# Rows for columns, an own-step product moved by one slot, and two units of batch two loaded ahead of the last weights, in a fused recurrence and MLP-mixer kernel

## The chip, the cores and the metric

The kernel runs on one core of a Trainium2 chip. The metric is device microseconds of one execution. Executions of one kernel spread: those of the kernel before by 0.6%. Runs are marked slow because they lie over 1.5% above the fastest run of their kernel; the medians below are over all runs of a kernel. Engines: PE multiplies matrices (PEld is its weight load), DVE, ACT and POOL work elementwise, SP issues most transfers. In the profile nearly every line is L68, a helper that issues all operations, so groups are told apart by their tiles.

## The reference, cut to what matters

Four batches, eight heads, 768 steps, head size 48. First a linear recurrence with a decay `w` and a bonus `u` for the own step, then a token mix and a channel mix.

```python
for t in range(S):
    cur = einsum('bhd,bhe->bhde', u * k_t, v_t)
    y[:, :, t] = einsum('bhd,bhde->bhe', r_t, state + cur)
    state = w * state + einsum('bhd,bhe->bhde', k_t, v_t)
x = y.transpose(0, 2, 1, 3).reshape(B, S, H * D)
h = relu(x.transpose(0, 2, 1) @ w_tok1) @ w_tok2
u = x + h.transpose(0, 2, 1)
out = u + relu(u @ w_ch1) @ w_ch2          # w_ch2: 1536 x 384
```

## The kernel before

The recurrence is cut into chunks of 128 steps. A *unit* is one chunk of one batch: units 0 to 5 are batch one, 6 to 11 batch two, and so on. A unit passes four stages, one per *slot*: `p` (elementwise products, on POOL for batch two and later), `a` (transposes), `b` (scores), `c` (output and state). Slot *s* runs `c` of unit *s*-3, `b` of *s*-2, `a` of *s*-1 and `p` of *s*, and each engine works through its instructions in program order. From batch two on, the slots are woven between the channel mix of the batch before: *ups* (u @ w_ch1, 0.5 us each) and *downs* (@ w_ch2, 2 us each).

```python
def load_unit(b, c):                     # k, r, v of one unit, 192 KB each, on SP
    ...
    if (b, c) in after and nm == "kt":   # hold the load back behind this instruction
        tc.add_manual_dep(ins.ins, after[b, c].ins.name, ...)

for q in range(2):                       # decay columns, element by element
    act.dma_start(wd[q * P:q * P + D, :], w.rearrange("(a q) d -> q d a", q=2)[q])
WARM = (10, 2, 1)                        # dummy products that keep PE's clock up
BY_POOL = (3, 5)                         # units of batch one whose kp POOL makes
WEIGHTS_AT = {4: (0,), 5: (1,), 6: (2,), 7: (3, 4)}   # 4 = all of w_ch2
...
def stage_p(b, c):                       # for b > 0: kp, rp, ku, all on POOL
    pool.tensor_mul(kp[:, :, 0:D], h3(kt), h3(wn[:, g, :]))   # kp: one of three buffers
    pool.tensor_mul(L["rp"][:, :, 0:D], h3(rt), h3(wp[:, g, :]))
    pool.tensor_mul(L["ku"], kt, u_bc)
def own_step(L):                         # yd, on POOL; in slot b for b > 0, in slot c for b == 0
    pool.tensor_mul(h3(L["yd"]), h3(L["vb"]), L["adg"]...)
...
after[1, 0] = done[0, C - 1]             # batch two's loads wait for batch one's last output
u1 = ups(0, 1)
items = ups(0, 0, 6) + u1[:6] + downs(0, 0, 0, 1) + u1[6:] + downs(0, 0, 1) + downs(0, 1)
events = [att(0.5, 6), att(4.0, 7)]      # slots 6, 7 at these places among the items
events += [att(8.0 + 3.2 * j, 8 + j) for j in range(7)]
events += mixing(1, 28.5, 31.5, 34.0)
merge(items, fetch([0.0] * 6 + ...) + events)
```

## Time and profile before

| | before |
|---|---|
| time | 185.99 us, median of 3 (185.12 to 186.02) |
| span of the profiled run | 184.1 us |
| batch one's attention ends (last `x_b`) | 31.75 us |
| products of unit 6 can start on POOL in full (`rp`) | 46.48 us |
| POOL's `kp` of unit 9 | 56.33 us |
| POOL's `rp` of unit 13 ends | 74.5 us |
| first up of batch two | 84.43 us |

The chain of waits of the kernel before follows. It is traced back from the last instruction; its columns are start, length, and what ran or was waited for.

```profile
1.74 5.33 DMA wd<-in_w_dram
7.16 0.21 ACT lnwd L68
...
10.07 0.16 PE at_ps_268 L68
...
31.19 0.56 DVE x_b L68
...
32.19 14.15 DMA rt<-in_r_dram
46.48 1.00 POOL rp_661 L68
...
56.37 0.96 POOL kp_139 L68
57.33 0.96 POOL rp_661 L68
58.28 1.12 POOL ku L68
59.52 0.83 POOL yd L68
...
73.23 1.28 POOL rp_663 L68
...
81.94 2.35 DMA uT<-u_sb
...
84.43 1.14 PE z_ps L68 x6
```

The chain has four parts: a start that waits for the decay columns, batch one's attention, 14 us of waiting for r of unit 6, then POOL at four operations per unit (about 4.0 us) until unit 13. After 84 us it is PE nearly without a break.

The list of waits of the kernel before (engine and tile that waited, releaser: total us, times, longest us):

```profile
POOL kp_139 L68 <- DMA kt<-in_k_dram: 11.5, 1, 11.5
...
DVE x_b L68 <- POOL yd L68: 5.6, 5, 1.8
...
POOL rp_661 L68 <- DMA rt<-in_r_dram: 3.1, 1, 3.1
```

Windows of five microseconds of the kernel before (window, its length, busy time and instruction count of PE, PEld, DVE, ACT and POOL, granted PE clock, DMA share, GB/s):

```profile
40.00:45.00 5.00, 3.00 (x21) 1.59 (x18) 0.00 (x0) 3.13 (x8) 0.99 (x1) 1.00 1.27 193
45.00:50.00 5.00, 2.48 (x11) 1.46 (x12) 1.44 (x2) 1.82 (x3) 3.52 (x4) 0.70 0.92 184
```

PE is busy 5.5 of these 10 us, the DMA engines are full, and the clock falls. This gap is what the change aims at: unit 6 lands behind the second channel weights (`w_ch2`), which landed at 46.1 us.

### The profile page before, as it was taken

To read this page: it belongs to the slowest core of one execution; us is meant where nothing else is said; L and a number is where in the kernel's file an instruction comes from. 1 tells how busy PE (TensorE), PEld (TensorE's weight loads), DVE (VectorE), ACT (ScalarE), POOL (GpSimd) and SP (SyncE) were. 2 spreads that over 40 slices of the span, in tenths; PEclk is the share of its full clock that TensorE was granted. 3 is DMA by queue.
4 is the path that set the end of the run, shared out by engine and by line. 5 is a ranking of instruction groups with operands and counts; after the bars stand their busy time and mean duration, and the time that the engine had idled before them with its cause. 6 is when DMAs were issued, how large, how long until landed. Compare 5 with 4: busy or idle time off the path is not lost.

```text
span 184.1 us, 3991 instructions
## 1 busy us (share of the span) xinstructions
PE 165.5 (90%) x1504; PEld 106.8 (58%) x1504; DVE 106.0 (58%) x193; ACT 100.0 (54%) x217; POOL 93.8 (51%) x113
## 2 busy tenths in 40 slices
PE   7788888893699899798999999899999999999992
PEld 2376776461367566465667666666665665656651
DVE  6465877700469999974669977996541071121121
ACT  2695565493578744404959748654645444445500
POOL 5459795002999999943597999991100000000000
PEclk9999999999699999999999999999999999999999
DMA  4999998999999998124699999233011134211212
GB/s 92 185 203 163 191 141 143 196 184 196 187 219 215 234 225 195 45 45 107 136 235 232 189 243 196 44 67 108 0 46 43 43 86 89 85 43 43 85 47 85
DMA packets 90354, 24.44 MB, mean 133 GB/s; under 512 B 83680, under 2 KB 90336, under 8 KB 90336
## 3 DMA queue, kind: packets, MB, share of 16 engines
q1 hardware_dynamic: 86368, 20.85, 54.0%
q0 software_dynamic: 3408, 3.15, 11.0%
q10 hardware_dynamic: 560, 0.20, 0.7%
q8 instruction: 12, 0.20, 0.4%
q14 instruction: 6, 0.05, 0.1%
HBM read 20.84 MB, written 4.72 MB: 139 GB/s over the span
## 4 chain that ended last, share of the span: by engine, by line
PE 58%; POOL 14%; DMA 13%; DVE 6%; ACT 5%; issue 3%; ACTq 0%; SPq 0%; DVEq 0%; POOLq 0%
PE h_ps L68 23%; PE z_ps L68 20%; DMA rt<-in_r_dram 8%; POOL ku L68 3%; POOL yd L68 3%; DMA wd<-in_w_dram 3%; PE tr_ps L68 3%; DMA uT<-u_sb 3%; PE y_ps L68 2%; PE ad_ps L68 2%; POOL rp_661 L68 2%; POOL rp_663 L68 1%; PE hT_ps L68 1%; POOL rp_665 L68 1%; DVE u_sb L68 1%
## 5 line engine op out<-in xcount | busy, mean ns | idle before, releaser
L68 ACT ACTIVATE zr<-z_ps 128x384 bf16<-128x384 f32 x96 | 44.3, 495 | 31.7 <-PE z_ps L68 31.6
L68 PE MATMUL h_ps<-wch_198,zr 128*128 128x384 bf16 x288 | 50.4, 326 | 0.2
L68 PEld LDWEIGHTS <-zr 128*128 128x128 bf16 x288 | 28.0, 98 | 18.9 <-issue 1.0
L68 DVE TENSOR_TENSOR osb<-u_sb,h_ps 128x384 f32<-128x384 bf16 x24 | 13.3, 552 | 44.5 <-PE h_ps L68 44.5
L68 ACT COPY rk<-tr_ps 128x1024 bf16<-128x1024 bf16 x18 | 18.2, 1012 | 19.2 <-PE tr_ps L68 18.7
L68 PE MATMUL z_ps<-uT,wch_0_196 128*128 128x384 bf16 x144 | 27.6, 337 | 1.1 <-DMA uT<-u_sb 1.1
L68 PE MATMUL z_ps<-uT,wch_1_197 128*128 128x384 bf16 x144 | 26.5, 326 | 0.8 <-ACT zr L68 0.6
L68 DVE TENSOR_TENSOR rku<-ku,rt 128x384 f32<-128x384 f32 x18 | 18.6, 1033 | 11.3 <-POOL ku L68 11.3
L68 POOL TENSOR_TENSOR yd<-vb,adg 128x384 f32<-128x384 bf16 x24 | 20.0, 834 | 7.3 <-DVE adg L68 6.7
L68 PEld LDWEIGHTS <-wch_0_196 128*128 128x128 bf16 x144 | 14.0, 101 | 10.4 <-issue 3.2
L68 POOL TENSOR_TENSOR ku<-kt,u_bc 128x384 f32<-128x384 f32 x18 | 20.0, 1110 | 0.0
L68 PEld LDWEIGHTS <-wch_1_197 128*128 128x128 bf16 x144 | 13.8, 98 | 10.1 <-issue 1.7
L68 DVE TENSOR_TENSOR x_b<-y_ps,yd 128x384 bf16<-128x384 f32 x24 | 13.3, 553 | 10.6 <-POOL yd L68 5.6
L68 POOL TENSOR_TENSOR kp_139<-kt,wn 128x384 bf16<-128x384 f32 x7 | 7.0, 999 | 17.2 <-DMA kt<-in_k_dram 11.5
L68 PEld LDWEIGHTS <-rk 48*128 48x128 bf16 (+1 forms) x272 | 11.4, 95 | 6.3 <-issue 3.0
L68 DVE TENSOR_TENSOR u_sb<-x_b,hT_ps 128x384 bf16<-128x384 bf16 x24 | 11.8, 547 | 1.5 <-PE hT_ps L68 1.5
L68 ACT CAST vb<-vt 128x384 bf16<-128x384 f32 x24 | 12.3, 514 | 0.0
L68 DVE TENSOR_REDUCE adg<-rku 128x8 f32<-128x384 f32 x18 | 9.9, 553 | 0.8
L68 PE MATMUL hT_ps<-h1r,wtok_195 128*128 128x384 bf16 x48 | 9.4, 326 | 0.9 <-ACT h1r L68 0.8
L68 PE MATMUL idle_ps<-warm 128*128 128x512 bf16 x20 | 7.8, 520 | 2.2 <-DVE warm L68 1.3
L68 PE MATMUL h_ps<-x_b,wtok_194 128*128 128x384 bf16 x48 | 8.9, 325 | 0.1
L68 POOL TENSOR_TENSOR rp_661<-rt,wp 128x384 bf16<-128x384 f32 x6 | 6.6, 1101 | 3.1 <-DMA rt<-in_r_dram 3.1
(318 smaller groups left out, 253.6 us busy)
## 6 DMA issues: line engine op xcount, KB each, us to landing
kt<-in_k_dram SPq DMA_DIRECT2D x24, 192.0 KB, 3.7
vt<-in_v_dram SPq DMA_DIRECT2D x24, 192.0 KB, 3.9
out_dram<-osb SPq DMA_DIRECT2D x24, 192.0 KB, 1.9
rt<-in_r_dram SPq DMA_DIRECT2D x18, 192.0 KB, 3.9
wch_198<-in_moe_w_ch_dram POOLq DMA_DIRECT2D x1, 1152.0 KB, 17.6
wch_0_196<-in_moe_w_ch_dram POOLq DMA_DIRECT2D x1, 576.0 KB, 8.9
wch_1_197<-in_moe_w_ch_dram POOLq DMA_DIRECT2D x1, 576.0 KB, 10.5
wtok_194<-in_moe_w_tok_dram POOLq DMA_DIRECT2D x1, 384.0 KB, 7.5
```

The lines of the kernel that those rows point to most:

```text
L68: return lambda *args, **kw: tc.keep_in_program_order(f(*args, **kw))
```

## The change

Its intent has three parts. The decay columns come as contiguous rows and one small transpose on PE, and in batch one `kp` goes to DVE and the own-step product `yd` moves into slot `b`, where its sums are made (the *front*). Units 6 and 7 are loaded ahead of the second channel weights, which are cut in two and issued after unit 7's products on POOL; slot times are shifted to suit (the *load order*). Batch two's token mix turns half its chunks by PE instead of by DMA and puts one of two rectified halves on DVE (the *turns*).

```diff
-    for q in range(2):
-        act.dma_start(wd[q * P:q * P + D, :], w.rearrange("(a q) d -> q d a", q=2)[q])
+    act.dma_start(rows_wu[0:HP]..., w.rearrange("(a q) d -> a q d", q=2))
+    act.dma_start(rows_wu[HP:HP + 3], u...)
...
-    WARM = (10, 2, 1)
+    WARM = (4, 4, 2, 1)
...
     keep_warm(WARM[0])
+    pe.transpose(wu_ps, rows_wu, ident_f[0:HP + 3, 0:HP + 3])
+    keep_warm(WARM[1])
...
-    WEIGHTS_AT = {4: (0,), 5: (1,), 6: (2,), 7: (3, 4)}
+    WEIGHTS_AT = {4: (0,), 5: (1,), 6: (2,), 7: (3,)}     # 4, 5: halves of w_ch2
...
-    BY_POOL = (3, 5)
+    BY_POOL = ()
...
             act.copy(L["adg"], ad_ps)
+            own_step(L)                                    # stage b; gone from stage c
...
+        if s == 7:
+            after[1, 0] = done[0, C - 2]
...
-    after[1, 0] = done[0, C - 1]
...
-        hid, bk, _ = token_mix(b)
+        hid, bk, tn = token_mix(b, by_pe=range(3) if b == 1 else ())
...
-    events = [att(0.5, 6), att(4.0, 7)]
-    events += [att(8.0 + 3.2 * j, 8 + j) for j in range(7)]
-    events += mixing(1, 28.5, 31.5, 34.0)
+    events = [att(0.0, 6), att(3.0, 7), (3.1, 0.0, lambda: load_weights((4, 5))), att(6.5, 8)]
+    events += [att(t, 9 + j) for j, t in enumerate((15.5, 19.0, 22.0, 25.0, 27.5, 30.0))]
+    events += mixing(1, 30.5, 32.5, 35.0)
```

## The prediction

> **What bounds the kernel now** (185.99 us, span 184.1)
>
> 1. Prologue: in the chain of waits the decay-column load (4-byte elements) takes 5.3 us; its logarithm starts at 7.16 us, the first score matmul at 10.0.
> 2. Batch one's attention, to 31.75 us: slots of about 3.7 us. The waits list puts DVE 5.6 us behind the own-step product `yd` on POOL, which stands behind the next unit's `m` and so behind the loads of r (landing near 6.9, 9.9, 12.9, 15.9, 19.5, 22.8 us). Windows show the DMA engines full.
> 3. 42.6 to 47.5 us: PE nearly idle (waits: POOL 11.5 us on k of unit 6, 3.1 on r). Unit 6 lands at 46.3 us, behind the second channel weights (46.1); the granted clock then falls to 0.5 for 3.4 us.
> 4. 46.5 to 74.5 us: the chain is POOL, 3.9 us per unit. To 84.4 us: token mix, ending in a 2.35 us DMA transpose.
> 5. Then PE is 98% busy (windows); only a shift helps.
>
> **The change, costed**
>
> - Contiguous rows and a transpose: first score matmul up to 2 us earlier.
> - `yd` in its slot, no `kp` on POOL in batch one: 3.5 us off the attention by compute. But the first token weights, issued after `m` of unit 4 (r landing 19.5) and 7.5 us in flight, land near 28 us and hold the mix. I take 2 us: attention ends near 29.7.
> - Units 6 and 7 ahead: r lands near 38 and 41 us. The second channel weights, issued on POOL after three operations of unit 7 (near 43 us), need about 3 us to start (as before) and share with queued unit loads. The Trainium skill ("DMA: Bandwidth & Descriptors", Queues, rings and completion order) says each engine goes round-robin between queues; the packet records agree: these weights moved 147 KB/us, the unit loads 37. Each half (590 KB) takes 4 us: landings near 51 and 55 us.
> - PE reaches the first down product, which needs both halves, near 45 us. The gap moves and grows to 7 to 9 us. Behind it in PE order stand six ups (3 us), a down (2 us), then slot 9; POOL's `kp` of unit 9 needs slot 9's `kv` product (three buffers): near 60 us, against 56.4. From there POOL's 3.9 us per unit rules: loss 2 to 5 us. The 2 us won earlier don't help.
> - PE transposes, one rectified half on DVE, one more down before the mix: from unit 13's last POOL product to the first up 8.2 us instead of 9.95, gain 1.75.
>
> Net: -1.75 plus 2 to 5; later PE idle may give 1. The second half's landing carries the error: at 50 us the change gains 2 us, at 55 it loses 3. That this schedule was picked suggests early; I shade down.
>
> **Predicted 186.5 us, 182 to 191 (8 in 10). Faster by over 2%: 0.2; within 2%: 0.5; slower: 0.3.**
>
> **Would show it right:** logarithm of the columns before 5.5 us; attention of batch one ending 1.5 to 3.5 us earlier; PE waiting 4 us or more for the weights' halves; POOL idle before `kp` of unit 9, ended by `kv`; the weights' DMA in the chain of waits; no DMA transpose in the chain before batch two's ups.
>
> **Would make it wrong:** the second half landing before 49 us (up to 3% faster); the clock falling twice (slower still); attention ending before 28 us with token weights in time.

## The result, and the profile after

The change is slower: 195.12 us, median of 4 runs (193.01 to 195.86), against 185.56 us (184.98 to 186.02). The ratio is 1.0499, 95% interval 1.0402 to 1.0595. Ratios here are the mean time of one kernel's fast runs over the mean of the other's fast runs of the same rounds, so not quite the ratio of the medians. (For some runs below the record's ratio is not that of the runs that it marks fast. With those alone it is 1.034 for the dummy products, 1.023 for the earlier issue and 0.998 for the added output buffers; the others move by under 0.1%.)

| | before | after |
|---|---|---|
| logarithm of the columns starts | 7.16 | 6.48 |
| first score matmul | 10.0 | 10.94 |
| batch one's attention ends | 31.75 | 30.07 |
| `rp` of unit 6 on POOL | 46.48 | 39.39 |
| second channel weights landed | 46.1 | 52.4 and 56.4 |
| POOL's `kp` of unit 9 | 56.33 | 64.83 |
| POOL's `rp` of unit 13 ends | 74.5 | 83.95 |
| first up of batch two | 84.43 | 93.84 |
| span | 184.1 | 194.0 |

The chain of waits of the kernel after:

```profile
2.36 3.71 DMA rows_wu<-in_u_dram
...
6.21 0.24 PE wu_ps L68
6.44 2.67 PE idle_ps L68 x6
...
10.94 0.21 PE at_ps_265 L68
...
27.48 10.80 DMA kt<-in_k_dram
38.43 0.65 POOL kp_137 L68
...
44.53 0.82 POOL wch_0_194 L68
45.35 11.03 DMA wch_1_195<-in_moe_w_ch_dram
56.42 2.08 PE h_ps L68 x6
58.49 4.14 PE z_ps L68 x18
62.63 1.96 PE h_ps L68 x12
...
69.80 0.96 POOL kp_139 L68
...
82.67 1.28 POOL rp_659 L68
...
84.39 3.42 PE h_ps L68 x12
...
93.84 2.11 PE z_ps L68 x12
```

Unit 6 is indeed on POOL 7 us earlier. But the chain now goes through the weights (11.03 us), then through the last six products of the first down, six ups and the second down, which all stand ahead of slot 9 in PE's order, and only then to POOL. In the kernel before only the first down stood there: slot 9's `kv` ran at 54.92 us, right behind it. The new slot time of 15.5 put the six ups and the second down ahead of slot 9 as well, and they took 6.1 us. Eighteen products of the ups took 4.14 us here; at full clock six ups are 2.9 us.

The list of waits of the kernel after:

```profile
POOL kp_137 L68 <- PE kv_ps L68: 20.7, 2, 14.2
...
PE h_ps L68 <- DMA wch_0_194<-in_moe_w_ch_dram: 6.4, 1, 6.4
...
PE h_ps L68 <- DMA wch_1_195<-in_moe_w_ch_dram: 1.9, 1, 1.9
```

POOL in order of time, in the kernel after, at `kp` of unit 9 (start, length, instruction, and in brackets the idle time before it and its releaser):

```profile
64.83 1.01 POOL L68 TENSOR_TENSOR kp_137<-kt,wn 128x384 bf16<-128x384 f32 x1 [14.19 <-PE kv_ps L68]
```

Windows of five microseconds of the kernel after:

```profile
45.00:50.00 5.00, 0.97 (x6) 0.39 (x4) 0.67 (x2) 2.06 (x6) 4.99 (x7) 1.00 1.03 144
50.00:55.00 5.00, 2.10 (x6) 0.87 (x7) 0.00 (x0) 0.00 (x0) 0.64 (x1) 0.56 1.27 185
55.00:60.00 5.00, 3.58 (x12) 1.68 (x12) 0.55 (x1) 0.49 (x1) 0.00 (x0) 0.50 1.01 198
```

PE stands still for most of 46 to 56 us, and POOL from 50.6 to 64.8 us: its wait of 14.2 us in the list. The DMA engines are full all the while. The clock was granted at 0.5 from 50.6 to 60.8 us, and once more from 84.7 to 88.1 us, in the token mix, where twelve products took 3.42 us.

### The profile page after: what moved, and what is told of

It reads as the page before. It is cut to its first block, busy times and chain, and to the rows that moved or that the text cites. A ratio compares the mean times of both kernels' runs of the same rounds, so it can differ in the third digit from the quotient of the medians.

```text
span 194.0 us, 4005 instructions
## 1 busy us (share of the span) xinstructions
PE 168.9 (87%) x1512; PEld 108.4 (56%) x1512; DVE 106.5 (55%) x197; ACT 101.4 (52%) x219; POOL 91.9 (47%) x111
## 3 DMA queue, kind: packets, MB, share of 16 engines
HBM read 20.84 MB, written 4.72 MB: 132 GB/s over the span
## 4 chain that ended last, share of the span: by engine, by line
PE 58%; DMA 14%; POOL 10%; DVE 9%; issue 3%; ACT 2%; DVEq 0%; POOLq 0%; ACTq 0%
PE h_ps L68 24%; PE z_ps L68 20%; DMA wch_1_195<-in_moe_w_ch_dram 6%; DMA kt<-in_k_dram 6%; POOL ku L68 2%; PE tr_ps L68 2%; PE y_ps L68 2%; DMA rows_wu<-in_u_dram 2%; PE idle_ps L68 2%; POOL rp_659 L68 2%; PE hT_ps L68 2%; POOL yd L68 2%; DVE rk L68 1%; POOL kp_139 L68 1%; DVE rku L68 1%
## 5 line engine op out<-in xcount | busy, mean ns | idle before, releaser
L68 PE MATMUL h_ps<-wch_0_194,zr 128*128 128x384 bf16 x144 | 28.3, 334 | 7.2 <-DMA wch_0_194<-in_moe_w_ch_dram 6.4
L68 PE MATMUL h_ps<-wch_1_195,zr 128*128 128x384 bf16 x144 | 28.3, 334 | 1.9 <-DMA wch_1_195<-in_moe_w_ch_dram 1.9
L68 ACT COPY rk<-tr_ps 128x1024 bf16<-128x1024 bf16 x18 | 18.2, 1012 | 15.0 <-PE tr_ps L68 14.0
L68 PEld LDWEIGHTS <-wch_1_193 128*128 128x128 bf16 x144 | 14.2, 101 | 11.1 <-issue 3.2
L68 POOL TENSOR_TENSOR kp_137<-kt,wn 128x384 bf16<-128x384 f32 x6 | 6.3, 1049 | 29.0 <-PE kv_ps L68 20.7
L68 POOL TENSOR_TENSOR ku<-kt,u_bc 128x384 f32<-128x384 f32 x18 | 19.2, 1069 | 0.0
L68 DVE TENSOR_TENSOR rku<-ku,rt 128x384 f32<-128x384 f32 x18 | 15.9, 886 | 5.9 <-POOL ku L68 5.9
L68 PE MATMUL h_ps<-x_b,wtok_190 128*128 128x384 bf16 x48 | 10.4, 364 | 0.1
L68 PE MATMUL idle_ps<-warm 128*128 128x512 bf16 x18 | 7.3, 517 | 1.4 <-DVE warm L68 1.4
```

Source lines behind the costliest of these rows:

```text
L68: return lambda *args, **kw: tc.keep_in_program_order(f(*args, **kw))
```

## The experiments

The theory: the load order alone costs the time, because the late weights stop PE at the first down, slot 9 stands behind it in program order, and POOL's chain stands behind slot 9. The rivals: the front costs it (the front rival), or the falls of the clock do (the clock rival). Four kernels ran side by side first, three rounds each.

### Load order undone

Edits are given against the kernel after, unless said otherwise.

```diff
-    WEIGHTS_AT = {..., 7: (3,)}
+    WEIGHTS_AT = {..., 7: (3, 4, 5)}
-            after[1, 0] = done[0, C - 2]       # in slot 7
+    after[1, 0] = done[0, C - 1]               # after the loop
-    events = ...                                # slot times of after
+    events = ...                                # slot times of before
```

> The kernel after with the load order alone undone: both halves of the second channel weights again issued in slot 7, batch two's loads again behind them, slot times of before. Order theory (the late weights hold the first down product, and with it slot 9 and POOL): the 9.5 us go, and the 1.7 us by which batch one's attention ends earlier stay; POOL starts r of unit 6 near 45 us; 183 to 185.5 us. Front rival (columns by transpose, kp on DVE, own-step product moved cost the time): it stays near 194. Clock rival (the second fall of the clock comes from something else): it stays above 190.

Measured: 186.77 us, ratio 1.0012 (0.9964 to 1.0059). The loss went, so it lay in the load order (loads and slot times together; no run parts the two). But the gain that I expected of the front did not come. The chain of waits of this kernel shows where it went:

```profile
28.91 0.56 DVE x_b L68
...
29.91 16.08 DMA rt<-in_r_dram
46.13 1.00 POOL rp L68
```

Attention ends 2.3 us earlier than in the kernel before (29.47 against 31.75 us), but r of unit 6 is there at 46.1 us as before (46.5): the wait for it grew from 14.2 to 16.1 us. The DMA engines are full all through this stretch (mean busy share above 1 in every window from 30 to 46 us, 163 to 188 GB/s), which fits a load that lands when its turn comes.

### Load order alone, on the kernel before

```diff
# against the kernel before
-    wch2 = wts.tile([128, NJ, dm], ...)
+    wch2 = [wts.tile([128, NJ // 2, dm], ...) for i in range(2)]
+    # weights after unit 7's products, batch two's loads from slot 7, slot times of after
```

> The kernel before with the load order alone changed: weights split in two and issued after unit 7's products, batch two's loads from slot 7, slot times of after; columns, own-step product and transposes as before. Order theory: second half lands near 57 us, POOL's kp of unit 9 starts near 65 us, two falls of the clock; 193 to 197 us. Front rival: 184 to 187 us.

Measured: 196.33 us, ratio 1.0495 (1.0423 to 1.0567), as much as the whole change. In its trace `kp` of unit 9 starts at 63.65 us, again released by `kv`:

```profile
63.65 1.00 POOL L68 TENSOR_TENSOR kp<-kt,wn 128x384 bf16<-128x384 f32 x1 [12.93 <-PE kv_ps L68]
```

The front rival falls.

### Downs behind slot 9

```diff
-    items = ups(0, 0, 6) + u1[:6] + downs(0, 0, 0, 1) + u1[6:] + downs(0, 0, 1) + downs(0, 1)
+    items = ups(0, 0, 6) + u1 + downs(0, 0) + downs(0, 1)
-    ... enumerate((15.5, 19.0, ...
+    ... enumerate((12.9, 19.0, ...
```

> The kernel after, loads unchanged, but PE's order changed: all up products of batch one's second half and slot 9 come ahead of the first down product. Order theory: the weights land as late (near 56 us), but kp of unit 9 no longer stands behind them and starts when its own load lands, 50 to 57 us instead of 64.8; 185 to 189 us. If the late weights themselves are the cost wherever the downs stand, it stays at 193 to 196 us.

Measured: 193.47 us, ratio 1.0336 (1.0256 to 1.0416): just better than the load order alone in the same rounds (1.0423 to 1.0567), and far less so than I expected. Slot 9 was set free: `rp` of unit 9 runs at 55.4 us instead of 65.8. But slot 10 still stood behind three downs, so POOL waited 5.6 us for its `kv` product, and `kp` of unit 10 started at 63.71 us (69.75 in the kernel after). The store of an output then stood in the chain of waits for 4.71 us from 61.48 us, and POOL waited 3.1 us more before `kp` of unit 11 (70.51 us). I had moved one link of the chain and counted as if I had moved all of them. The first up of batch two came at 90.9 us, 3 us earlier than after.

### Dummy products in the wait

```diff
-    items = ups(0, 0, 6) + u1[:6] + downs(0, 0, 0, 1) + ...
+    items = ups(0, 0, 6) + u1[:6] + [(0.0, lambda: keep_warm(44))] + downs(0, 0, 0, 1) + ...
```

> The kernel after with 44 dummy products ahead of the first down product (9.4 us at full clock), so that PE isn't idle while it waits. Clock rival (the fall of the clock in and after the wait is the main cost): 186 to 189 us. Order theory: only the 2 us by which six downs and eighteen ups run slower at half clock come back, perhaps 1.5 us more at the token mix; kp of unit 9 still starts at 62 to 64 us; 191 to 194 us.

Measured: 194.26 us (just above the range named; two of the four runs are marked slow, and the two fast ones, 192.19 and 193.27 us, lie in it), ratio 1.0421 (1.034 to 1.0502). The chain of waits of this kernel:

```profile
45.42 9.44 PE idle_ps L68 x43
54.86 1.95 PE h_ps L68 x12
56.81 2.92 PE z_ps L68 x18
59.74 1.95 PE h_ps L68 x12
```

The same ups now take 2.92 us, and the two downs 1.95 us each. Yet `kp` of unit 9 starts only at 61.94 us: PE still comes to the downs at 54.86 us. So the clock is a part, some 2 us, and not the main cause. (The intervals of this run and of the load order alone overlap, so by times alone the gain is not certain; the trace shows it.) A fall of the clock remained, from 72.2 to 75.6 us.

The next four kernels ran together, three rounds each.

### Weights in two steps, a version built on the theory

```diff
-    items = ups(0, 0, 6) + u1[:6] + downs(0, 0, 0, 1) + ...
+    items = ups(0, 0, 6) + u1 + downs(0, 0)                 # last three downs go to batch two
-    events = [...]
+    events = [att(0.0, 6), att(2.9, 7), (3.0, 0.0, lambda: load_weights((4,)))]
+    events += [att(5.8, 8), att(8.7, 9), (8.8, 0.0, lambda: load_weights((5,)))]
+    events += [att(t, 10 + j) for j, t in enumerate((11.6, 14.5, 17.4, 20.8, 24.2))]
+    events += mixing(1, 25.6, 27.6, 30.0)
-    WARM = (4, 4, 2, 1)
+    WARM = (10, 1, 2, 1)
```

> A version built on the order theory: from the kernel after, half 0 of the weights is issued after unit 7's products and half 1 after unit 9's, all up products and slots 6 to 12 come ahead of the first down, the last three downs go into batch two's up products, and ten warming products instead of four stand before the transpose. Order theory: POOL's units follow one another from near 40 us at about 3.9 us each with no gap over 3 us, r of unit 13 ends near 70 us instead of 83.9, and the kernel beats both: 178 to 184 us. If the DMA engines cannot bring units 9 to 12 in time beside the weights, POOL waits for k and r instead: 184 to 188 us.

Measured: 185.73 us, ratio 0.9993 (0.9916 to 1.0071). The whole loss is gone with the two units still ahead, so the load order can be borne if PE's order goes with it. But it gains nothing over the kernel before: POOL waits 2.6 us for k of unit 11, and the clock was at 0.5 three times, 3.41 us each, from 28.0, 48.5 and 62.2 us. That these two are the reason is not shown.

### Weights issued ahead of unit 7's products

```diff
-    events = [att(0.0, 6), att(3.0, 7), (3.1, 0.0, lambda: load_weights((4, 5))), ...
+    events = [att(0.0, 6), (1.4, 0.0, lambda: load_weights((4, 5))), att(3.0, 7), ...
```

> The kernel after with the weights issued on POOL ahead of unit 7's three products instead of behind them. Order theory: issue near 41.3 us instead of 44.5, both halves land and kp of unit 9 starts some 3 us earlier (near 61.5 us), the time falls by 2 to 4 us to 191 to 193.5 us, since the landing rules PE, and unit 7's later products don't.

Measured: 191.6 us, ratio 1.0339 (1.0256 to 1.0422). The median is in the range named; two of the four runs are marked slow, and the two fast ones, 189.22 and 190.79 us, lie below it. The issue came at 39.1 us instead of 44.5, the second half was used at 51.0 us instead of 56.4, and `kp` of unit 9 started at 58.6 us instead of 64.8:

```profile
58.60 1.00 POOL L68 TENSOR_TENSOR kp<-kt,wn 128x384 bf16<-128x384 f32 x1 [10.14 <-PE kv_ps L68]
```

What moves the weights' landing moves POOL by about as much: 5.4 and 6.2 us. (I had expected 3 us; the issue itself moved by 5.4. From landing to slot 9's `kv` it took 7.2 us instead of 8.0; the fall of the clock lasted 3.41 us instead of 10.24.)

### Weights never loaded

```diff
-    (3.1, 0.0, lambda: load_weights((4, 5))),
+    (3.1, 0.0, lambda: [dve.memset(t, 0.0) for t in wch2]),
```

> The kernel after with the second channel weights never loaded but set to zero on DVE at the place of their issue (wrong result on purpose; no down product waits for a transfer). Order theory: no stall at the first down, slot 9 near 52 us, kp of unit 9 starts at 50 to 53 us, r of unit 13 ends at 69 to 72 us; 179 to 183 us: what the intent would bring if the weights cost nothing. If the cost lay in the shifted slots or in POOL or DVE work, it stays above 190 us.

Measured: 183.54 us, ratio 0.988 (0.9811 to 0.995). Its output is wrong, which doesn't matter for the time. The stall goes with the transfer, and `kp` of unit 9 starts at 52.67 us, as expected. The time is just above the range named. Its chain of waits shows that the intended gain was small from the start:

```profile
52.42 0.18 PE kv_ps L68 x4
52.67 1.00 POOL kp L68
...
69.66 1.28 POOL rp L68
...
71.60 3.53 PE h_ps L68 x11
```

Even with nothing to wait for, PE reaches slot 9 only at 52.4 us, as six ups and two downs stand ahead of it, and POOL waits 4.8 us. Then the clock falls in the token mix (0.5 from 69.9 to 76.7 us) and eleven products take 3.53 us. So with weights that cost nothing this schedule would win 1.2%. (The run also read 2.36 MB less from memory, 18.48 MB instead of 20.84, so part of this may come from emptier DMA queues.) It shows too that the new slot times cost nothing where the weights don't have to be waited for.

### Four kp buffers

```diff
-    NB = 3
+    NB = 4
```

> The kernel after with four buffers for kp and rp instead of three. If the kp buffer alone is what holds POOL (as my prediction said): three products of unit 9 run ahead near 56 us and the rest of POOL's chain follows 3 us earlier, 190 to 192.5 us. If slot 9 holds POOL in any case, through the own-step sums of the next slot on DVE (yd of unit 8 at 69 us): kp of unit 9 runs near 55 us but kp of unit 10 still starts at 69 to 70 us, 193 to 196 us.

Measured: 195.28 us, ratio 1.0426 (1.0306 to 1.0546). POOL in order of time, in the kernel with four buffers (start, length, instruction, and in brackets the idle time before it and its releaser):

```profile
50.79 0.98 POOL L68 TENSOR_TENSOR kp<-kt,wn 128x384 bf16<-128x384 f32 x1
...
68.68 0.83 POOL L68 TENSOR_TENSOR yd<-vb,adg 128x384 f32<-128x384 bf16 x1 [14.81 <-DVE adg L68]
69.47 1.00 POOL L68 TENSOR_TENSOR kp<-kt,wn 128x384 bf16<-128x384 f32 x1
```

The buffer was a gate, but not the only one: unit 9's products ran 14 us earlier, and POOL then waited as long for the own-step sums of unit 8, which stand behind slot 9's work on DVE. `kp` of unit 10 started at 69.47 us against 69.75. The gate is slot 9 as a whole; my prediction named one of its two doors.

The last runs had five rounds each, for differences below one per cent.

### No dependency, weights in slot 7

```diff
-    WEIGHTS_AT = {..., 7: (3,)}
+    WEIGHTS_AT = {..., 7: (3, 4, 5)}
-            after[1, 0] = done[0, C - 2]
-    items = ups(0, 0, 6) + u1[:6] + downs(0, 0, 0, 1) + ...
+    items = ups(0, 0, 6) + u1 + downs(0, 0) + downs(0, 1)
+    # slots 8 and 9 at 11.0 and 15.0, then 18.5 ... 30.0
```

> A version built on what the runs showed: the kernel after, but all second channel weights issued in slot 7 as before, and batch two's loads held back by nothing, so that they take their round-robin share beside the weights from about 21 us on; all up products ahead of the first down. Order theory: r of unit 6 lands near 35 to 38 us, the weights near 47 us, PE doesn't stall for them by more than 2 us, kp of unit 9 starts at 52 to 54 us (56.4 before), r of unit 13 ends near 71 us; 181.5 to 184.5 us. If the loads delay the token weights and so the mix by more than 1.5 us: 185 us and above.

Measured: 186.1 us, ratio 1.0044 (0.9998 to 1.0091). The time is that of the second branch of the expectation, but its reason is there only in part: the token weights took 8.1 us (7.0 in the kernel after) and the token mix started at 28.65 us (27.88), a delay of 0.8 us and not of over 1.5. POOL's chain did start earlier (`kp` of unit 9 at 55.0 us), but the clock fell at 29.7 and at 74.1 us, and it came to nothing; why is not shown.

### The front alone

```diff
# against the kernel before: columns by transpose, kp and the diagonal on DVE, yd in stage b;
# weights, dependency, slot times and token mix as before (the weights in two tiles, issued together)
```

> The kernel before with only the first two parts of the change: columns by one transpose, own-step product in the slot of its sums (kp and the diagonal on DVE). Order theory: batch one's attention ends 1.5 to 2.5 us earlier, but r of unit 6 lands at 46 us as before, behind the same weights, and the time is the same as before within 0.6%. If the front were on the critical path: 1.7 to 2.5 us faster, 183 to 184 us.

Measured: 184.25 us, ratio 0.995 (0.9906 to 0.9995). Its chain of waits:

```profile
30.45 13.84 DMA rt<-in_r_dram
44.43 0.99 POOL rp L68
```

Attention ends 1.7 us earlier, and in the profiled run r of unit 6 was there 2 us earlier than before, not at 46 us as I had written. In the run with the load order undone, which differs from this one only in the turns (they come later), it was there at 46.1 us. So how much of the front's gain gets through the full DMA queues varies between two runs that should not differ up to there; in time it is half a per cent here.

### Two steps with the clock kept up, and more output buffers

```diff
# against the two-step version
+    events = [(t, 0.0, lambda: keep_warm(5)) for t in (2.9, 5.8, 8.7, 11.6, 14.5, 17.4)]
-    WARM = (10, 1, 2, 1)
+    WARM = (4, 4, 2, 1)
# the second of the two runs has in addition
-    osb = mpool.tile([128, dm], f32, name="osb")
+    osb = mpool.tile([128, dm], f32, name="osb", bufs=4)
```

> The version with the weights in two steps, with five dummy products in each of six slots where PE waited for POOL, and the warming products of after. Clock theory for that version (three falls of 3.4 us at half clock): one fall at most in the span from 28 to 80 us, and 1 to 3 us less, 182.5 to 184.5 us. If POOL and the loads rule there whatever the clock: 185 to 186.5 us.

Measured: 184.28 us, ratio 0.992 (0.9875 to 0.9965). The clock stayed at full speed from 11.9 us to the end of the work. One run of six (188.7 us) is marked slow. The intervals of this version and of the one without dummies overlap, so what the clock is worth in it stays open.

> The version with the weights in two steps and dummy products, with four output buffers instead of two: in its trace an output add on DVE waited for an earlier output's store (3.8 us in the chain near 67 to 70.6 us), which stands on the DMA queue behind unit loads. If that wait is on the path: 182.5 to 183.8 us. If the unit loads set the pace of that stretch whatever DVE does: as without it, 184 to 185 us.

Measured: 185.21 us, ratio 1.0016 (0.9969 to 1.0064). The ratio shows no gain from the buffers. That fits the second branch: the unit loads set the pace, and not the output store. This run holds the clock as well (mean granted clock 1.0) and has the two-step order too, yet shows no gain. I therefore don't claim that the two-step version beats the kernel before; what it may gain lies below one per cent.

## Why the prediction was right or wrong

The mechanism was right in direction; the size and the final number were wrong. The prediction said 186.5 us (182 to 191); measured 195.12 us. The step that failed is the cost of the path from the weights' landing to `kp` of unit 9 ("near 60 us ... loss 2 to 5 us"): that stretch took 8.4 us where 5 were counted, the landing came 1.4 us late, and the gain of 1.75 us that was to set it off did not come (9.9 us as before).

What held:

- *Landings.* Predicted near 51 and 55 us, measured 52.4 and 56.4. The Trainium skill ("DMA: Bandwidth & Descriptors", Queues, rings and completion order) says that each engine goes round-robin between its queues. The trace's packet records (one for each row moved) agree: from 48 to 55 us of the kernel after, 1296 rows of the weights and 1401 of the unit loads, 142 KB/us against 38, as the weights' rows are four times as large (768 and 192 bytes).
- *The gate.* PE waited 8.3 us for the halves (6.4 + 1.9; 4 or more was the test), POOL's idle time before `kp` of unit 9 was ended by `kv`, the weights' transfer was in the chain, and no DMA transpose stood before batch two's ups. The load order alone and its undoing show that the load order, loads and slot times together, is the whole loss (ratios 1.0495 and 1.0012); the earlier issue shows that POOL follows the landing. No run has the late weights with the old slot times. With slot 9 right behind the first down, as before, its `kv` would have come up to 6.1 us earlier (an estimate from the 4.14 and 1.96 us that the six ups and the second down took); the run with the downs behind slot 9 warns that the next slots might then have held the chain.
- *The end of batch one's attention.* 1.7 us earlier; predicted about 2.

What failed, term by term. Measured at the first up of batch two, the loss is 9.4 us (84.43 to 93.84); the sum of the prediction was -1.75 plus 2 to 5.

- *"`kp` of unit 9 ... near 60 us ... loss 2 to 5 us."* It was 64.83 us, a loss of 8.5. The landing was 1.4 us later. From there to slot 9's `kv` took 8.0 us (56.42 to 64.42), where I had counted 5: I left out the last six products of the first down (1 us), and the clock stood at 0.5 until 60.8 us, so those six took 2.08 us and the six ups 4.14 instead of 2.9. The dummy run shows the stretch at full clock: 1.95, 2.92 and 1.95 us. The Trainium skill ("TensorE: Matmul & The Clock Gate", Part 1: The HAM clock gate) says that the clock is halved after an idle window of about 3.4 us. The clock records agree for the fall at 50.6 us: PE had then stood idle for 4.6 us, and the fall lasted 10.24 us, three times 3.41. They do not for the fall of 3.41 us at 84.7 us: PE had been busy for 2.0 of the 3.41 us before it, with no gap over 0.9 us. I had predicted a wait of 7 to 9 us myself and had seen the fall after the old gap, and still costed the work behind the wait at full clock; I named a second fall only among the things that could go wrong.
- *POOL's pace.* From `kp` of unit 9 to the end of unit 13's `rp` it took 19.1 us instead of 18.2; 1.2 us of it is the wait for the sums of unit 8.
- *"From unit 13's last POOL product to the first up 8.2 us instead of 9.95, gain 1.75."* It took 9.9 us as before (83.95 to 93.84), while the clock fell again at 84.7 us. In the run with four buffers, where the clock stayed up there, the same stretch took 8.7 us (83.66 to 92.32). So about 1.25 us of the gain is real at full clock.
- *"That this schedule was picked suggests early; I shade down."* This step took off 1 to 2 us against my own count, on no evidence in the trace.
- *"Logarithm of the columns before 5.5 us", "first score matmul up to 2 us earlier".* 6.48 us, and the matmul came 0.9 us later. The rows took 3.71 us from issue to landing; PE idled 2.9 us before the transpose, its full clock came at 9.6 us instead of 6.1, and six dummies behind the transpose took 2.67 us on the path. The end of attention was still 1.7 us earlier; whether the later start cost anything is not shown.

What stays open: the share of the clock in the loss is not cleanly separated by times (1.0421 against 1.0495, intervals overlap); how the loss divides between the late weights and the later place of slot 9; and whether a version with the units ahead can beat the kernel before by more than a per cent. None of the four that I built clearly did.

## What to carry to other kernels

In this kernel, whose DMA engines were full, moving one load ahead of another moved the wait to the other; follow the delayed load to the first in-order instruction that needs it, and list everything that stands behind that instruction on its engine and then on the others. Look at the granted clock behind a long PE wait (here 0.5 for 10.24 us after a wait of 6.4 us) and cost the work there by it; and cost all links: freeing slot 9 alone, or one buffer alone, left the chain where the next link held it. When slots are shifted to suit a late load, check what the shift itself puts ahead of them. A number that comes out of the trace should not be bent by a guess about why someone picked the schedule.

## What the Trainium skill lacked or had wrong

- "TensorE: Matmul & The Clock Gate" (Terms) gives the penalty as throttled time times (1 - K/N). For the 13.65 us at half clock in the kernel after that is an estimate of 6.8 us. With dummies, 3.41 us at half clock were left, an estimate of 5.1 us less; the first up of batch two came 4.1 us earlier, and against the load order alone in the same rounds the ratio fell only from 1.0495 to 1.0421 (1.034 by the runs marked fast, some 2.9 us). The formula came out too high here; PE stood idle for 3.7 of the 10.24 us of the first fall.
- "DMA: Bandwidth & Descriptors" (Queues, rings and completion order) describes the round-robin between queues, but not what follows for the bytes: here the two queues moved nearly equal counts of rows (1296 and 1401), so bytes went by row size, 142 against 38 KB/us at 768 and 192 bytes.
- The same page (Latency and other measured facts) gives about 1 us to the first byte of a transfer issued on POOL, without the moment from which it counts. Here the first packet came 2.0 us after the issuing instruction began and 1.1 us after it ended (44.47, 45.35 and 46.43 us, first half); for the token weights of the kernel before it came 3.0 and 2.0 us after (20.59, 21.61 and 23.60 us). Each issue held POOL for 0.8 to 1.0 us.
- "TensorE: Matmul & The Clock Gate" has no figure for how busy PE must be to keep its clock. Here it fell with PE busy, by the trace's records, for 2.0 of the 3.41 us before (kernel after, at 84.7 us) and for 2.7 of them (load order alone on the kernel before, at 19.1 us).
